# A two-layer H3 convolution and SwiGLU kernel: a list scheduler in the kernel orders all engines, and the first block is transformed without butterflies

## The chip, the cores and the metric

The kernel runs on one core of one Trainium2 chip. The time is the device time of one execution in microseconds (us). The core has five engines with a queue each, which they work off in order: TensorE (PE in the profile; its weight loads are shown apart as PEld), VectorE (DVE), ScalarE (ACT), GpSimd (POOL) and SyncE (SP), which here only starts transfers (DMA). They wait for each other by semaphores. Matmul results land in PSUM, which has eight banks of 128 x 512 fp32; all else lies in SBUF.

## What is computed

Two layers, each a gated long convolution followed by a SwiGLU network, both with a layer norm in front and a sum behind. S is 2048, D is 512, F is 1792, all in bf16. The reference, cut to what matters:

```
def A(q, k, v, shift_k, ssm_k, ssm_D):
    k_shift = causal convolution of k with 4 taps per channel
    kv = k_shift * v
    y = irfft(rfft(pad(kv)) * rfft(pad(ssm_k)))[:S]     # causal convolution over S
    return q * (y + kv * ssm_D)
def B(x, w_gate, w_up, w_down):
    return (silu(x @ w_gate) * (x @ w_up)) @ w_down
x = A_q
x = x + A(layernorm(x), A_k, A_v, ...);  x = x + B(layernorm(x), ...)
x = x + A(layernorm(x), A_k, A_v, ...);  x = x + B(layernorm(x), ...)
```

The convolution y does not depend on x, so it is computed once and used by both layers.

## The kernel before

**Tiles.** The sequence is cut into four blocks of 512 rows (NB), each held as 128 partitions x 4 rows (R). The tokens of a block are worked in two halves of 2 x 128 rows. A *unit* is (layer, block, half); the 16 units run block by block, (0,c,0), (0,c,1), (1,c,0), (1,c,1).

**The convolution** of a block c: hn (the kernel's taps) is transposed on TensorE into hs; the shift convolution is 64 matmuls of kTb with the diagonal taps dg, and VectorE multiplies the result into vt (L216). A transform of hs or vt goes to the frequency domain in two steps: eight sums of two matmuls each with the cosine and sine blocks fwd, evicted by ScalarE into ev (`half`, L160 to L169), and then butterflies of sums and differences on VectorE (L174, L175), which give X (of vt) or H (of hs). G is H combined with the H of the block before. `product` (L224) multiplies X and G in four slots of two parts, into Z. `inverse` (L253) first folds Z by sums and differences into su (L250, L251), then runs four sums of four matmuls with inv, one for each row r, and ScalarE copies them to Yk. Blocks 1 to 3 also need products with earlier blocks.

**A prologue** of a unit (L310): layer norm statistics of xc (L290, L291), ve = variance + eps (L294) and rstd = ve to the power -1/2 (L296) on GpSimd, n (L302), times Yk, added to xc, a second layer norm in the same way, z (L302), and z transposed into zT: by DMA on SyncE's queue (L335), for the very first unit on TensorE (L333).

**A unit's network**: `gate_up` (L343) has 112 matmuls of 256 columns of zT with wg and wu into the PSUM banks pf; ScalarE evicts them to sg (silu) and ht, VectorE multiplies (L358). `down` (L368) has 28 matmuls of ht with wd into two banks pd, which VectorE adds to xc (L380). For layer 1, xc is then stored (L366).

**What sets the order.** Up to the first unit the order of VectorE, ScalarE and TensorE is that of the code. Behind it, the units' loop has a hook, `tick`, after each pair of gate and up tiles: it draws steps from the next units' prologues and from a stream of convolution work, by two accounts of estimated cost (rates 2.8 and 1.2). The framework's own scheduler then places the instructions. Loads of hn and vt of block 0 go by ScalarE's queue, all others by SyncE's. TensorE begins with 36 matmuls of the identity that compute nothing (L459).

Of the kernel before, what the change touches and what calls it, by code (L numbers as in the profile page):

```python
# [18 lines left out]
NB = 4  # L19
R = 4  # L20
# [5 lines left out]
          ("nC", 1, 3), ("nC", 2, 3), ("S", 2, 0), ("S", 3, 0)]  # L26
BI = {(f, r): i for i, (f, r, _) in enumerate(BLOCKS)}


@with_exitstack  # L30
def kernel(
# [20 lines left out]
    N = 2 * L  # L52
    assert L == R * P and D == KD * P and F == NF * P and D <= 512

    q2 = A_q.rearrange("b s d -> (b s) d")
    k2 = A_k.rearrange("b s d -> (b s) d")
    v2 = A_v.rearrange("b s d -> (b s) d")
    o2 = out.rearrange("b s d -> (b s) d")

    q_t = q2.rearrange("(c p r) d -> p c r d", p=P, r=R)  # L60
    v_t = v2.rearrange("(c p r) d -> p c r d", p=P, r=R)
    o_t = o2.rearrange("(c p r) d -> p c r d", p=P, r=R)
    k3 = k2.rearrange("s (dt p) -> s dt p", p=P)
    h3 = A_ssm_k.rearrange("(dt p) s -> p dt s", p=P)


    HP = R // 2
    FG = [range(f, min(f + 4, NF)) for f in range(0, NF, 4)]

    const = tc.alloc_tile_pool(name="const", bufs=1)  # L70
    ldp = tc.alloc_tile_pool(name="ld", bufs=1)
    big = tc.alloc_tile_pool(name="big", bufs=10)
    wp = tc.alloc_tile_pool(name="wts", bufs=1)
    xp = tc.alloc_tile_pool(name="xp", bufs=2)
    small = tc.alloc_tile_pool(name="small", bufs=4)
    work = tc.alloc_tile_pool(name="work", bufs=2)
    psp = tc.alloc_tile_pool(name="psp", bufs=1, space=PSUM)

    PADL = 16
    sig, xs, wts = {}, {}, {}  # L80

    def load_h(b, eng):
        hn = ldp.tile([P, KD, L], BF16, name="hn")
        eng.dma_start(out=hn[:], in_=h3[:, :, b * L:(b + 1) * L])
        sig[b, "h"] = hn

    def load_k(b):
        kTb = ldp.tile([P, KD, PADL + L], BF16, name="kTb")
        if b == 0:
            nc.gpsimd.memset(kTb[:, :, 0:PADL], 0.0)  # L90
            nc.sync.dma_start_transpose(out=kTb[:, :, PADL:PADL + L], in_=k3[0:L])
        else:
            nc.sync.dma_start_transpose(out=kTb[:, :, :], in_=k3[b * L - PADL:(b + 1) * L])
        sig[b, "k"] = kTb

    def load_v(b, eng):
        vt = ldp.tile([P, R, D], BF16, name="vt")
        eng.dma_start(out=vt[:], in_=v_t[:, b])
        sig[b, "v"] = vt

    def load_x(c):
        xc = xp.tile([P, R, D], BF16, name="xc")
        nc.sync.dma_start(out=xc[:], in_=q_t[:, c])
        xs[c] = xc

    def load_weights(which):
        if which in ("g", "u"):
            t = wp.tile([P, KD, F], BF16, name=f"w{which}_sb")
            src = (B_w_gate if which == "g" else B_w_up).rearrange("(k p) f -> p k f", p=P)
        else:  # L110
            t = wp.tile([P, NF, D], BF16, name="wd_sb")
            src = B_w_down.rearrange("(k p) d -> p k d", p=P)
        nc.sync.dma_start(out=t[:], in_=src)
        wts[which] = t

    def psf():
        return psp.tile([P, D], F32, name="pf", bufs=4)

    def psc():
        return psp.tile([P, D], F32, name="pc", bufs=2)  # L120
# [5 lines left out]
    def drain(*gens):  # L126
        for g in gens:
            for _ in g:
                pass

    def together(*gens):
        gens = list(gens)
        while gens:
            for g in list(gens):
                if next(g, gens) is gens:
                    gens.remove(g)


    FWD_TERMS = {
# [5 lines left out]
    NT = len(BLOCKS)  # L145
    fwd = const.tile([P, NT, P], BF16, name="fwd")
    inv = const.tile([P, NT, P], BF16, name="inv")
    ident = const.tile([P, P], BF16, name="ident")
    tapT = const.tile([P, KD, KS], BF16, name="tapT")
    dcol = const.tile([P, KD, 1], BF16, name="dcol")  # L150
    dg = const.tile([P, KD, KS, P], BF16, name="dg")
    nhalf = const.tile([P, 1], F32, name="nhalf")

    def fT(f, r):
        return fwd[:, BI[f, r], :]

    def iT(f, r):
        return inv[:, BI[f, r], :]

    def half(rows, ev, par, scale, ps_of, engines):  # L160
        for key in ("ac", "bd")[par]:
            slot = "abcd".index(key)
            for part in (0, 1):
                ps = ps_of()
                mm(ps[:], [(fT(f, r), rows[:, r, :]) for f, r in FWD_TERMS[key][part]])
                if engines[part] is nc.vector:
                    nc.vector.tensor_scalar(out=ev[:, slot, part], in0=ps[:], scalar1=scale, scalar2=None, op0=ALU.mult)
                else:
                    nc.scalar.activation(out=ev[:, slot, part], in_=ps[:], func=ACT.Copy, scale=scale)  # L169
            yield 0, 0.9  # L170

    def butterfly(ev, dst, sl):
        lo, hi = (slice(0, 2), slice(2, 4)) if sl is None else (sl, sl + 2)
        nc.vector.tensor_tensor(out=dst[:, lo], in0=ev[:, lo], in1=ev[:, hi], op=ALU.add)  # L174
        nc.vector.tensor_tensor(out=dst[:, hi], in0=ev[:, lo], in1=ev[:, hi], op=ALU.subtract)  # L175

    def forward(rows, dst, scale):
        ev = big.tile([P, 4, 2, D], BF16, name="ev", tag="s8")
        for par in (0, 1):
            yield from half(rows, ev, par, scale, psc, (nc.scalar, nc.scalar))  # L180
        butterfly(ev, dst, None)
        yield 2.4, 0

    X, G, H, Y, Z = {}, {}, {}, {}, {}

    def transpose_h(b, ring, order=(0, 2)):
        hn = sig.pop((b, "h"))
        hs = ldp.tile([P, R, D], BF16, name="hs")
        sig[b, "hs"] = hs
        for r0 in order:  # L190
            pt = psp.tile([P, 2, D], BF16, name="pt", tag=ring[0], bufs=ring[1])
            for r in (r0, r0 + 1):
                for dt in range(KD):
                    nc.tensor.transpose(pt[:, r - r0, dt * P:(dt + 1) * P], hn[:, dt, r:L:R], ident[:])
            nc.scalar.copy(out=hs[:, r0:r0 + 2, :], in_=pt[:])  # L195
            yield 0, 0.5

    def spectrum_h(b):
        yield from transpose_h(b, ("pc", 2))
        H[b] = big.tile([P, 4, 2, D], BF16, name="H", tag="s8")  # L200
        yield from forward(sig.pop((b, "hs")), H[b], 2.0 / N)
        G[b] = big.tile([P, 4, 2, D], BF16, name=f"G{b}", tag="s8")
        Hp = H.pop(b - 1)
        nc.vector.tensor_tensor(out=G[b][:, :, 0, :], in0=H[b][:, :, 0, :], in1=Hp[:, :, 1, :], op=ALU.subtract)
# [19 lines left out]
    def product(i, j, sl=slice(0, 4)):  # L224
# [3 lines left out]
        if k not in Z:  # L228
            Z[k] = big.tile([P, 4, 2, D], BF16, name="Z", tag="s8")
# [343 lines left out]
```

## Time and profile before

| | |
|---|---|
| median of 3 runs | 409.09 us (408.4 to 410.74) |
| the profiled execution | 409.77 us |
| its span, first to last instruction | 408.0 us |
| mean granted TensorE clock | 0.97 |
| TensorE busy | 372.0 us |
| VectorE busy | 279.3 us |
| ScalarE busy | 188.9 us |
| GpSimd busy | 41.3 us |

All times that follow from rows are of the profiled execution; its span is 1.8 us below its own time and 1.1 us below the median. In a row of the timeline stand the start, the length, the engine, the line of the kernel, the operation with its tiles and shapes, the count, and in brackets the idle time before it with what ended it. Rows of one engine can overlap a little, since its instructions are pipelined.

### The profile page before, as it was taken

The page shows a single profiled execution, that of the slowest core. Times are in us where ns is not written, and L with a number is a line of the kernel's source. Part 1 is how long each engine was busy: PE and PEld are TensorE (multiplying, and loading weights), DVE is VectorE, ACT ScalarE, POOL GpSimd, SP SyncE. Part 2 cuts the span into 40 slices and gives each one's busy share as a digit, 9 for nine tenths or more (in the row PEclk, how much of TensorE's full clock was granted, in tenths as well). Part 3 has the DMA queues.
Part 4 walks back from the last instruction along what each step waited for, and adds up shares of the span by engine and source line. Part 5 has one row for each costly group of instructions (what it writes and reads, how often), then busy time and mean ns, then how long its engine had stood idle before and what let it go on. Part 6 is the DMA issues. An engine that isn't in the chain of part 4 may idle for free.

```text
span 408.0 us, 6771 instructions
## 1 busy us (share of the span) xinstructions
PE 372.0 (91%) x2808; PEld 266.2 (65%) x2808; DVE 279.3 (68%) x469; ACT 188.9 (46%) x319; POOL 41.3 (10%) x73
## 2 busy tenths in 40 slices
PE   4977699986999999999969989996999999999996
PEld 4832586754767677867646766784767577767773
DVE  5588791987998228978999981597889761445322
ACT  4496236432454553455415436631454444434451
POOL 1100100021011000020121220011010100000000
PEclk9799699998999999999999999998999999999999
DMA  8993030101012320202020112001010020020100
GB/s 213 399 266 129 3 73 20 40 0 27 0 27 52 79 79 0 55 8 71 2 51 2 27 39 66 2 2 26 2 26 27 7 58 17 0 27 0 27 27 26
DMA packets 34351, 20.42 MB, mean 50 GB/s; under 512 B 26384, under 2 KB 32272, under 8 KB 34320
## 3 DMA queue, kind: packets, MB, share of 16 engines
q1 hardware_dynamic: 32592, 18.93, 17.1%
q10 hardware_dynamic: 1728, 1.05, 1.0%
q8 instruction: 22, 0.36, 0.4%
q14 instruction: 9, 0.07, 0.1%
HBM read 11.80 MB, written 2.10 MB: 34 GB/s over the span
## 4 chain that ended last, share of the span: by engine, by line
PE 49%; DVE 32%; POOL 6%; DMA 5%; issue 4%; ACT 4%; ACTq 0%; DVEq 0%
PE pf L124 30%; PE pd L377 12%; PE pc L124 6%; DVE bnst L290 4%; DVE t L236 3%; POOL rstd L296 3%; DVE ht L358 3%; POOL ve L294 3%; DVE t L234 3%; DMA zT<-z 3%; DVE t L243 2%; DVE xc L380 2%; DVE Z L240 2%; DMA hn<-in_A_ssm_k_dram 2%; DVE n L302 2%
## 5 line engine op out<-in xcount | busy, mean ns | idle before, releaser
L355 ACT ACTIVATE sg<-pf 128x512 bf16<-128x512 f32 x112 | 66.9, 597 | 151.7 <-PE pf L124 135.9
L124 PE MATMUL pf<-zT,wg_sb 128*128 128x256 bf16 x896 | 119.4, 276 | 7.4 <-DMA zT<-z 7.4
L124 PE MATMUL pf<-zT,wu_sb 128*128 128x256 bf16 x896 | 118.4, 276 | 0.0
L377 PE MATMUL pd<-wd_sb,ht 128*128 128x512 bf16 x448 | 107.8, 379 | 8.7 <-DVE ht L358 7.0
L124 PEld LDWEIGHTS <-wg_sb 128*128 128x128 bf16 x896 | 88.3, 99 | 34.6 <-issue 5.8
L124 PEld LDWEIGHTS <-wu_sb 128*128 128x128 bf16 x896 | 88.9, 99 | 11.3
L358 DVE TENSOR_TENSOR ht<-ht,sg 128x1024 bf16<-128x1024 bf16 x64 | 39.4, 616 | 62.8 <-ACT ht L356 62.8
L356 ACT CAST ht<-pf 128x512 bf16<-128x512 f32 x112 | 65.7, 586 | 33.1 <-PE pf L124 33.1
L377 PEld LDWEIGHTS <-ht 128*128 128x128 bf16 x448 | 42.9, 98 | 53.3 <-DVE ht L358 10.5
L294 POOL TENSOR_SCALAR ve<-mv 128x2 f32<-128x2 f32 x32 | 17.6, 550 | 336.0 <-DVE mv L291 336.0
L290 DVE BATCH_NORM_STATS2 bnst<-xc 128x6 f32<-128x512 bf16 x64 | 41.5, 677 | 0.3
L380 DVE TENSOR_TENSOR xc<-xc,pd 128x512 bf16<-128x512 bf16 x32 | 20.9, 681 | 16.4 <-PE pd L377 16.4
L169 ACT ACTIVATE ev<-pc 128x512 bf16<-128x512 f32 x48 | 26.6, 600 | 2.9 <-PE pc L124 2.7
L234 DVE TENSOR_TENSOR t<-X,G 128x2048 bf16<-128x2048 bf16 (+1 forms) x22 | 24.6, 1118 | 0.3
L236 DVE TENSOR_TENSOR t<-X,G 128x2048 bf16<-128x2048 bf16 (+1 forms) x22 | 24.6, 1116 | 0.0
L296 POOL TENSOR_TENSOR rstd<-ve,nhalf 128x2 f32<-128x2 f32 x32 | 22.7, 710 | 2.7
L124 PEld LDWEIGHTS <-fwd 128*128 128x128 bf16 x128 | 12.7, 99 | 15.3 <-issue 6.5
L302 DVE TENSOR_SCALAR z<-xc,mv,rstd 128x512 bf16<-128x512 bf16 x32 | 11.8, 410 | 14.7 <-POOL rstd L296 14.7
L302 DVE TENSOR_SCALAR n<-xc,mv,rstd 128x512 bf16<-128x512 bf16 x32 | 11.8, 409 | 11.9 <-POOL rstd L296 11.9
L124 PEld LDWEIGHTS <-kTb 128*128 128x128 bf16 x256 | 17.8, 120 | 0.2
L124 PE MATMUL pc<-hs,fwd 128*128 128x512 bf16 x48 | 14.3, 411 | 1.1 <-ACT hs L195 0.9
L243 DVE TENSOR_TENSOR t<-t,t 128x2048 bf16<-128x2048 bf16 x12 | 14.6, 1215 | 0.1
(62 smaller groups left out, 226.6 us busy)
## 6 DMA issues: line engine op xcount, KB each, us to landing
xc<-in_A_q_dram SPq DMA_DIRECT2D x4, 512.0 KB, 3.8
out_dram<-xc SPq DMA_DIRECT2D x16, 128.0 KB, 1.7
wg_sb<-in_B_w_gate_dram SPq DMA_DIRECT2D x1, 1792.0 KB, 12.2
wu_sb<-in_B_w_up_dram SPq DMA_DIRECT2D x1, 1792.0 KB, 17.7
wd_sb<-in_B_w_down_dram SPq DMA_DIRECT2D x1, 1792.0 KB, 16.0
hn<-in_A_ssm_k_dram SPq DMA_DIRECT2D x3, 512.0 KB, 5.7
vt<-in_A_v_dram SPq DMA_DIRECT2D x3, 512.0 KB, 3.7
hn<-in_A_ssm_k_dram ACTq DMA_DIRECT2D x1, 512.0 KB, 7.7
```

Of the source, the lines that this page charges most:

```text
L124: nc.tensor.matmul(o, lhsT=lhsT, rhs=rhs, start=(n == 0), stop=(n == len(terms) - 1))
L234: nc.vector.tensor_mul(out=t1[:], in0=Xi[:, sl, 0, :], in1=Gj[:, sl, part, :])
L236: nc.vector.tensor_mul(out=t2[:], in0=Xi[:, sl, 1, :], in1=Gj[:, sl, 1 - part, :])
L290: nc.vector.bn_stats(out=st[:], in_=xc[:, HP * h + o, :])
L294: nc.gpsimd.tensor_scalar(out=ve[:], in0=mv[:, :, 1], scalar1=LN_EPS, scalar2=None, op0=ALU.add)
L296: nc.gpsimd.tensor_tensor(out=rstd[:], in0=ve[:], in1=nhalf[:].to_broadcast((P, HP)), op=ALU.pow)
L302: eng.tensor_scalar(out=dst, in0=xc[:, HP * h + o, :], scalar1=mv[:, o, 0:1], scalar2=rstd[:, o:o + 1], op0=ALU.subtract, op1=ALU.mult)
L355: nc.scalar.activation(out=sg[:, o:o + 2, :], in_=pg[:], func=ACT.Silu)
L356: nc.scalar.copy(out=ht[:, o:o + 2, :], in_=pu[:])
L358: nc.vector.tensor_mul(out=ht[:], in0=ht[:], in1=sg[:])
L377: nc.tensor.matmul(pd[:], lhsT=ht[:, q, o * P:(o + 1) * P], rhs=wts["d"][:, ft, :], start=(ft == 0), stop=(ft == NF - 1))
L380: nc.vector.tensor_add(out=xc[:, i, :], in0=xc[:, i, :], in1=pd[:])
```

## The change

The units' loop, `tick`, the stream and the framework's scheduling are taken out. Each step of the whole kernel is now added to a plan as an operation with an engine, an assumed cost, what it reads and writes and, for the network's steps, a due time. A list scheduler inside the kernel (`Plan.order`) lays down all five engines' orders at once, before anything is emitted: it plays the steps through with the assumed costs, takes on each engine the step that can start first, the one due first where several can start, and gives out buffers (rings of tiles by name) as they come free in that play. Due times: unit starts are laid 22 us apart (18 for the last block), from 38 us on; steps ahead get theirs from what waits for them.

Other parts of the change:

- The first block's X is computed without butterflies: `direct` puts the sum or difference into the choice of blocks, with four matmuls for each of eight results. Two more blocks of cosines and sines are held for it (14 in place of 12).
- Its product goes slot by slot: two operations of 1024 columns with one operand broadcast, two of 512.
- Its inverse, `inverse_direct`, has no fold: four PSUM banks (two named pd, two pc) collect 32 single matmuls as slots of Z come.
- ve is computed on VectorE, the power stays on GpSimd.
- The first unit's second layer norm goes row by row.
- The loads of hn and vt of block 0 go by SyncE's queue.
- Where TensorE would stand idle over 0.5 us before 38 us of the play, identity matmuls are put in: 120 in all.

The diff, cut to its core:

```diff
+    def order(self, warm_until, warm):
...
+        while done < len(self.ops):
+            best = None
+            for e, cand in ready.items():
...
+                    key = (max(est, t[e] + self.WAIT[e]), o.due, o.n)
+                    if pick is None or key < pick[0]:
+                        pick = (key, est, o)
+                if pick is not None and (best is None or pick[1] < best[1]):
+                    best = pick
...
+            if e == "PE" and est < warm_until and est - t[e] > 0.5:
+                self.dummy(warm, t[e], est)
...
+            o.emit()
+            o.start, o.end = est, est + o.cost
...
+    def direct(rows, dst, ring, engs):
+        for slot in (0, 2, 1, 3):
+            c1, c2, sign = (("a", "c", 1), ("b", "d", 1), ("a", "c", -1), ("b", "d", -1))[slot]
+            for part in (0, 1):
+                terms = FWD_TERMS[c1][part] + [(f if sign > 0 else NEG[f], r) for f, r in FWD_TERMS[c2][part]]
...
+                add("PE", pe(4), lambda ps=ps, terms=terms: mm(ps.t[:], [(fT(f, r), rows.t[:, r, :]) for f, r in terms]),
+                    r=[rows, fwd], w=[ps])
...
+        if n == 1:
...
+            for t, part in ((t1, 0), (t2, 1)):
+                dve(2 * D, lambda t=t, part=part: nc.vector.tensor_mul(
+                    out=t.t[:], in0=x.t[:, sl, part:part + 1, :].to_broadcast((P, 2, D)), in1=g.t[:, sl]),
...
+    def inverse_direct(k, slots_order):
...
+        pss = [new(("pd", "pd", "pc", "pc")[r], "ps", [P, D], F32) for r in range(R)]
+        for n, slot in enumerate(slots_order):
+            for part in (0, 1):
+                for r in range(R):
...
+                    st, sp = (n == 0 and part == 0), (n == len(slots_order) - 1 and part == 1)
+                    add("PE", pe(1), lambda f=f, q=q, r=r, slot=slot, part=part, st=st, sp=sp: nc.tensor.matmul(
+                        pss[r].t[:], lhsT=iT(f, q), rhs=z.t[:, slot, part], start=st, stop=sp),
...
-        nc.gpsimd.tensor_scalar(out=ve[:], in0=mv[:, :, 1], scalar1=LN_EPS, scalar2=None, op0=ALU.add)
+        add("DVE", 0.08, lambda: nc.vector.tensor_scalar(out=ve.t[:], in0=mv.t[:, :, 1], scalar1=LN_EPS, scalar2=None,
+                                                         op0=ALU.add), r=[mv], w=[ve])
...
+    T0, DF, DC = 38.0, 18.0, 22.0
...
+    plan.dues({"DVE": 2.0, "PE": 3.0, "ACT": 1.0, "POOL": 1.0, "SP": 1.0}, T0 + 2)
...
+        plan.order(T0, warm)
```

Three places show how the instructions move. The first is SyncE's queue at the start of the program, with its first loads. Before:

```order
L91 DMA_TRANSPOSE kTb<-in_A_k_dram 128x4x512
L103 DMA xc<-in_A_q_dram 128x2048
L113 DMA wg_sb<-in_B_w_gate_dram 128x4x1792
L113 DMA wu_sb<-in_B_w_up_dram 128x4x1792
L84 DMA hn<-in_A_ssm_k_dram 128x4x512
```

And in the same place of the changed kernel, where the first hn and vt are among them:

```order
L280 DMA_TRANSPOSE kTb<-in_A_k_dram 128x4x512
L274 DMA hn<-in_A_ssm_k_dram 128x4x512
L289 DMA vt<-in_A_v_dram 128x2048
L300 DMA wg_sb<-in_B_w_gate_dram 128x4x1792
L293 DMA xc<-in_A_q_dram 128x2048
L300 DMA wu_sb<-in_B_w_up_dram 128x4x1792
```

xc has moved from second place to fifth, behind hn, vt and wg; the hn of the first rows above is that of block 1.

The second place is VectorE in the first block: X, G and Z are its spectra, t the two halves of a product. Before:

```order
L174 TENSOR_TENSOR X_308<-evx 128x1024
L175 TENSOR_TENSOR X_308<-evx 128x1024
L234 TENSOR_TENSOR t_386<-X_308,G_309 128x1024
L236 TENSOR_TENSOR t_387<-X_308,G_309 128x1024
L240 TENSOR_TENSOR Z<-t_386,t_387 128x2x512
L234 TENSOR_TENSOR t_422<-X_308,G_309 128x1024
L236 TENSOR_TENSOR t_423<-X_308,G_309 128x1024
L240 TENSOR_TENSOR Z<-t_422,t_423 128x2x512
L250 TENSOR_TENSOR su<-Z 128x1024
L251 TENSOR_TENSOR su<-Z 128x1024
```

And the end of the same stretch in the changed kernel, up to the first prologue:

```order
L435 TENSOR_TENSOR t_503<-X_440,G_420 128x1024
L439 TENSOR_TENSOR Z<-t_465,t_476 128x512
L439 TENSOR_TENSOR Z<-t_483,t_494 128x512
L435 TENSOR_TENSOR t_520<-X_440,G_420 128x1024
L439 TENSOR_TENSOR Z<-t_483,t_494 128x512
L439 TENSOR_TENSOR Z<-t_503,t_520 128x512 x2
L553 TENSOR_TENSOR n<-n,Yk 128x512 x2
```

The butterflies of X and the folds to su are gone, and the products stand slot by slot.

The third place is VectorE from the end of the first unit's down projection, in the prologue of unit (1,0,0). Before:

```order
L380 TENSOR_TENSOR xc<-xc,pd 128x512 x2
L290 BN_STATS bnst<-xc 128x6 x2
L291 BN_AGGR mv<-bnst 128x2
L240 TENSOR_TENSOR Z<-t_1002,t_1003 128x4x512
L291 BN_AGGR mv<-bnst 128x2
L234 TENSOR_TENSOR t_1097<-X_742,G_309 128x2048
L302 TENSOR_SCALAR n<-xc,mv,rstd 128x512 x2
L358 TENSOR_TENSOR ht<-ht,sg 128x1024
L320 TENSOR_TENSOR n<-n,Yk 128x1024
L236 TENSOR_TENSOR t_1098<-X_742,G_309 128x2048
L321 TENSOR_TENSOR xc<-xc,n 128x1024
L243 TENSOR_TENSOR t_1097<-t_1097,t_1098 128x2048
```

And in the changed kernel:

```order
L612 TENSOR_TENSOR xc<-xc,pd 128x512 x2
L511 BN_STATS bnst<-xc 128x6 x2
L512 BN_AGGR mv<-bnst 128x2 x2
L600 TENSOR_TENSOR ht<-ht,sg 128x1024
L514 TENSOR_SCALAR ve<-mv 128x2
L446 TENSOR_TENSOR t_1042<-X_440,G_681 128x2048
L522 TENSOR_SCALAR n<-xc,mv,rstd 128x512 x2
L543 TENSOR_TENSOR n<-n,Yk 128x1024
L544 TENSOR_TENSOR xc<-xc,n 128x1024
L511 BN_STATS bnst<-xc 128x6 x2
L512 BN_AGGR mv<-bnst 128x2 x2
```

Of four products of 2048 columns between the sum and the second statistics, one is left; ve is a row of VectorE now.

More of the change, by code (lines that the diff above doesn't have):

```diff
@@ L184 @@
[L184 to L204, printed above, removed]
-        yield 1.2, 0
-        nc.vector.tensor_tensor(out=G[b][:, :, 1, :], in0=H[b][:, :, 1, :], in1=Hp[:, :, 0, :], op=ALU.add)
-        yield 1.2, 0
@@ new lines, with run, conv @@
+    spectrum_h(1, "pf")
+    inverse_direct(0, (0, 2, 1, 3))
+    prologue(0, 0, 0, True)
+    prologue(0, 0, 1)
+    T0, DF, DC = 38.0, 18.0, 22.0
+    start = {}
+    t = T0
+    order = [(layer, c, h) for c in range(NB) for layer in (0, 1) for h in range(HP)]
+    for unit in order:
+        start[unit] = t
+        t += DC if unit[1] < NB - 1 else DF
+    def run(unit):
+        ffn(unit, start[unit], DC if unit[1] < NB - 1 else DF)
+    def conv(c):
+        if c >= NB:
+            return
+        if c > 1:
+            spectrum_h(c)
+        spectrum_x(c)
+        load_x(c)
+        if c + 1 < NB:
+            load_h(c + 1)
+            load_k(c + 1)
+            load_v(c + 1)
+        product(0, c)
+        product(c, 0)
+        inverse(c)
```

911 lines of the change are left out of this document (522 added, 389 removed), and 4 rows, old and new, of the table INV_TERMS.

## The prediction

> **What bounds the kernel now.** I read the page first, then the chain of work that ended last, then the timeline, and last the windows in which TensorE stood idle. The page's first part:
>
> ```profile
> span 408.0 us, 6771 instructions
> PE 372.0 (91%) x2808; PEld 266.2 (65%) x2808; DVE 279.3 (68%) x469; ACT 188.9 (46%) x319; POOL 41.3 (10%) x73
> ```
>
> TensorE (PE) looks nearly full, but a modelled busy time hides slow stretches. So I price its work by pieces of the chain that ran without a gap (start, length, count):
>
> ```profile
> 54.15 0.89 PE pc L124 x16
> 55.05 1.75 PE pf L124 x16
> 56.79 0.89 PE pc L124 x16
> 57.69 1.73 PE pd L377 x8
> ```
>
> That is 0.056 us for a matmul of 128 columns, 0.109 for 256, 0.216 for 512. From the first gate matmul on, the kernel of before runs 1792 of 256 (195.4 us), 448 of 512 for the down projections (96.9) and, for the later blocks' convolutions, 208 of 128 (11.6) and 128 of 512 (27.7): 331.6 us. Between which times?
>
> ```profile
> 46.48 1.92 PE L124 MATMUL pf<-zT,wg_sb 128*128 128x256 bf16 x8
> ...
> 403.90 1.28 DVE L380 TENSOR_TENSOR xc<-xc,pd 128x512 bf16<-128x512 bf16 x2 [1.11 <-PE pd L377]
> ```
>
> The gate starts at 46.5; VectorE (DVE) takes up the last sum at 403.9, so the matmuls end there: 357.4 us for 331.6 of work. The span is a ramp of 46.5, work of 331.6, **25.8 lost**, and a tail of 4.1 that stays. The losses are gaps such as these and slow restarts behind them (after the range: its length, then each engine's busy time, PE first, DVE third):
>
> ```profile
> 80.00:100.00 20.00, 15.09 (x98) 9.90 (x97) 18.08 (x29) 4.86 (x9) 4.83 (x5) 0.93 0.07 14
> 200.00:220.00 20.00, 15.86 (x107) 10.00 (x106) 18.57 (x29) 7.17 (x13) 3.62 (x4) 1.00 0.10 26
> 260.00:280.00 20.00, 17.23 (x155) 12.98 (x153) 18.19 (x31) 6.27 (x11) 3.08 (x4) 1.00 0.04 8
> ```
>
> In each, TensorE misses 3 to 5 us while VectorE is over 90% busy; over the span VectorE is at 68%. It serves convolution products while a prologue that TensorE needs stands in line: a matter of order, not of amount.
>
> **The ramp.** Before:
>
> ```profile
> 21.24 3.63 PE L124 MATMUL pf<-vt,fwd 128*128 128x512 bf16 x16
> 22.12 4.07 ACT L169 ACTIVATE evx<-pf 128x512 bf16<-128x512 f32 x8
> ...
> 24.26 0.69 DVE L174 TENSOR_TENSOR X<-evx 128x1024 bf16<-128x1024 bf16 x1 [0.67 <-ACT evx L169]
> ...
> 36.94 0.68 DVE L251 TENSOR_TENSOR su<-Z 128x1024 bf16<-128x1024 bf16 x1
> ```
>
> From 24.26 to 37.62 VectorE runs 20 operations of 1024 columns, 0.67 us apart. The change takes away four butterflies of X and four folds (8 x 0.67 = 5.3 us), and gives TensorE 16 more forward and 16 more inverse matmuls (32 x 0.216 = 6.9 us). The product becomes, for each of four slots, two operations of 1024 columns (0.61 each, the step inside a run of such rows) and two of 512 (0.37, half of this row): about 2.0 us, 8.0 in all.
>
> ```profile
> 43.48 0.73 DVE L302 TENSOR_SCALAR z<-xc,mv,rstd 128x512 bf16<-128x512 bf16 x2 [1.14 <-POOL rstd L296]
> ```
>
> A slot of X takes TensorE 8 x 0.216 = 1.73 us, less than VectorE's 2.0, so the added forward matmuls lie beside VectorE but for the first slot: 1.73, and 0.8 until it is evicted, 2.5. The inverse matmuls follow as slots come; only the last two of the first two rows are on the path.
>
> When can the direct transform start? It needs vt multiplied, and here the loads matter (last column: from issue to landing):
>
> ```profile
> 2.19 0.74 SPq L103 DMA_DIRECT2D xc<-in_A_q_dram  x1
> ...
> 2.99 0.41 SPq L113 DMA_DIRECT2D wg_sb<-in_B_w_gate_dram  x1
> ```
> ```profile
> wg_sb<-in_B_w_gate_dram SPq DMA_DIRECT2D x1, 1792.0 KB, 12.2
> ...
> xc<-in_A_q_dram SPq DMA_DIRECT2D x1, 512.0 KB, 8.4
> ```
>
> xc landed at 10.6, wg at 15.2. Now xc stands behind hn, vt and wg on one queue; the five first loads are the same 3.9 MB, so I put xc near 14.8, where wg ended. VectorE has three statistics of xc ahead of the first vt multiply, and waits there.
>
> ```profile
> 18.81 1.25 DVE L216 TENSOR_TENSOR vt<-pf,vt 128x512 bf16<-128x512 f32 x2
> ```
> ```profile
> 78.40 1.20 DVE bnst L290 x2
> ```
>
> Four statistics (0.60), four multiplies (0.62), two n (0.37) and small ones make 5.9 us: vt is done at 20.7, against 20.1 before. The h transform's evictions (0.51 each) run behind it to about 22.9. So 22.9 + 2.5 + 8.0, less 0.4 since the last slot waits for TensorE: **Z is done at 33.0**, against su at 37.6. From su to the gate before took 8.9 us. Now: two matmuls and evictions 1.3, multiply and add by row 1.4, two statistics and ve 1.7, two powers 1.7, z, transposes and eviction 1.3, together 7.4. **The gate starts at 40.4, a gain of 6.1.**
>
> Both ends of what no row shows: xc landing at 10.6 brings 3.5 us; a broadcast operand that halved the product's rate would cost eight times 0.53, 4 us. The dummy matmuls, 113 now ahead of hn's transposes, are the third:
>
> ```profile
> 1.72 2.95 PE L459 MATMUL pf<-ident 128*128 128x128 bf16 x26 [1.72 <-POOL ident masks.py:199]
> ```
> ```profile
> 4.25 1.16 PE L459 MATMUL pf<-ident 128*128 128x128 bf16 x12
> ```
>
> At the first row's pace, 0.106 us, they hold TensorE to 13.7, 4 us too long; in the second the pace is 0.08 and falling. At 0.056 from 4.9 on they end at 9.5, when hn's transposes began before. I take 9.5, as the later row is nearer to what follows.
>
> **The units.** After the gate TensorE has 332.9 us of work by the same prices (16 shift and two inverse matmuls more). How much of the 25.8 comes back? A layer-1 unit's gate waits for a chain: the down projection two units earlier, the add to xc, two layer norms, a transpose by DMA.
>
> ```profile
> 77.12 1.27 DVE L380 TENSOR_TENSOR xc<-xc,pd 128x512 bf16<-128x512 bf16 x2
> ...
> 96.05 1.03 PE L124 MATMUL pf<-zT,wg_sb 128*128 128x256 bf16 x8 [2.17 <-DMA zT<-z]
> ```
> ```profile
> 192.18 1.28 DVE L380 TENSOR_TENSOR xc<-xc,pd 128x512 bf16<-128x512 bf16 x2
> ...
> 211.02 1.03 PE L124 MATMUL pf<-zT,wg_sb 128*128 128x256 bf16 x8 [1.24 <-DMA zT<-z]
> ```
>
> Both took 18.9 us, and in both the order puts 13.6 us of VectorE work between add and second z: a chain needs its VectorE work and 5.2. TensorE's work between that down projection and the gate, counted in the order, is the room. Before, for the eight layer-1 units: room 14.8, 19.1, 17.4, 15.4, 16.6, 16.5, 13.9, 13.9; VectorE work 13.6, 14.2, 9.6, 13.6, 16.0, 8.5, 7.9, 7.9. What is missing is 4.0, 0.3, 0, 3.4, 4.6, 0, 0, 0, in sum 12.3, and 25.8 were lost: about twice, with restarts and the other units in it. Now: room 15.7, 18.3, 13.9, 16.5, 17.4, 15.7, 15.7, 15.7; work 10.4, 12.7, 10.4, 10.4, 11.5, 10.4, 8.1, 8.1. Missing is 1.7 in one unit; five others fit with under 1 us to spare. Twice 1.7, and 1.6 for the tight ones: **5 us lost in place of 25.8.** The ends are 0 and all of 25.8.
>
> Loads on SyncE (SP) were read for waits: a load that waits for its buffer stands ahead of zT transposes in four places, but its buffer is freed over 10 us of TensorE work ahead of those gates, so it costs nothing; if TensorE came later than its order says, the gate would move with it.
>
> ve moves from GpSimd (POOL) to VectorE, 33 times 0.1 us there. Beside a product it had cost more:
>
> ```profile
> 48.21 0.22 POOL L294 TENSOR_SCALAR ve<-mv 128x2 f32<-128x2 f32 x1 [4.77 <-DVE mv L291]
> ...
> 80.96 1.16 POOL L294 TENSOR_SCALAR ve<-mv 128x2 f32<-128x2 f32 x1 [31.74 <-DVE mv L291]
> 82.20 0.71 POOL L296 TENSOR_TENSOR rstd<-ve,nhalf 128x2 f32<-128x2 f32 x1
> ```
>
> The slow ve began 0.14 us behind a product of 1.2 and ended with it. Now the power stands in that place: in 10 of 33 the row behind ve is a product. I take it that the power is held as ve was: the 5.2 has that in it, so nothing is gained, and where nothing holds it some 0.3 a norm is hidden. If it is not held, the 5 us fall to about 2. The Trainium skill, GPSIMD Engine Reference, section Key points, says that GpSimd shares its SBUF interfaces with VectorE and contends with its instructions of two SBUF inputs; the slow row agrees, and by that rule the sum stays at 5 us lost, against 2 without it.
>
> **Sum.** 40.4 + 332.9 + 5 + 4.1 = 382.4 us of span. The profiled execution of before took 409.77 for 408.0, and the median is 409.09, 1.1 above the span: 383.5.
>
> **Rivals.** (1) *The waits stay.* The order is laid by assumed costs, and an engine that comes late holds its whole queue. For it: five rooms with under 1 us to spare. Against: the four chains that had been too long have 12 us less work. All 25.8 lost gives 404.3; half, 391. (2) *The ramp gains less*, by the late xc, slow dummies or the broadcast: gate at 44.4, 387.5; all of it at 46.5, 389.6. (3) *Slower: the power is locked out by a run of products, not one.* If GpSimd got in only when VectorE pauses, each of 33 powers could wait another 1.14 us, 38 us, and the time would be 421; it ends above 409 from 0.78 us each on. Against it: the slow ve ended with one product, and VectorE itself stops for rstd. (4) *Nothing*: rooms and ramp gains cancel, 407 to 411.
>
> **How the numbers follow.** Forecast 377 to 387: 0.57. Ramp rival, 387 to 391: 0.15. Waits stay, 391 to 407: 0.21. No change: 0.03. Slower: 0.04. So faster by over 0.5% (about what a measurement of this kernel can tell from no change) 0.93, same 0.03, slower 0.04. The range 376 to 399 holds forecast, ramp rival and the lower half of the waits, a little over 8 in 10; its low end has an early xc and under 2 us lost.
>
> **What would show it.** First gate matmul near 40, Z done near 33, and bnst of xc late in the ramp, waiting for a DMA; windows behind the gate with TensorE gaps of some us in all, and no wait over 2 us for zT; gate to last matmul near 338 us. A gate after 44, or a wait of ht or zT in every unit, would make it wrong.

## The result, and the profile after

The changed kernel took 388.21 us (median of 4 runs, 387.24 to 389.45) against 409.29 us for the kernel before in the same comparison: a ratio of 0.948, 95% interval 0.9445 to 0.9522. The forecast was 383.5 us, in a range of 376 to 399. The profiled execution took 387.24 us, its span 385.5 us; the mean granted TensorE clock rose from 0.970 to 0.995.

The page's first part; TensorE does not do much less (the transforms cost more matmuls), it idles less:

```profile
span 385.5 us, 6975 instructions
PE 369.3 (96%) x2883; PEld 268.6 (70%) x2926; DVE 282.7 (73%) x504; ACT 189.1 (49%) x320; POOL 35.7 (9%) x42
```

The same three windows of 20 us as before, with the engines' busy times in the same order. Where TensorE missed 3 to 5 us, it now misses 0.4 to 0.5, although VectorE is fuller than it was (the worst window behind the gate is now that from 100 to 120 us, in which TensorE misses 1.5):

```profile
80.00:100.00 20.00, 19.57 (x153) 14.87 (x153) 19.28 (x28) 9.13 (x17) 2.87 (x2) 1.00 0.07 14
200.00:220.00 20.00, 19.62 (x149) 13.88 (x150) 18.62 (x32) 11.91 (x20) 2.45 (x3) 1.00 0.11 27
260.00:280.00 20.00, 19.50 (x146) 14.29 (x147) 19.76 (x33) 9.01 (x16) 3.65 (x3) 1.00 0.07 14
```

The timeline of the changed kernel, cut to the steps of the ramp and the last sum:

```profile
1.73 8.53 PE L733 MATMUL wm<-ident 128*128 128x128 bf16 x113 [1.73 <-POOL ident masks.py:199]
...
16.57 1.29 DVE L511 BATCH_NORM_STATS2 bnst<-xc 128x6 f32<-128x512 bf16 x2 [4.73 <-DMA xc<-in_A_q_dram]
...
21.82 0.68 DVE L395 TENSOR_TENSOR vt<-ps,vt 128x512 bf16<-128x512 f32 x1
...
24.98 7.07 PE L252 MATMUL ps<-vt,fwd 128*128 128x512 bf16 x32
...
31.40 1.29 DVE L435 TENSOR_TENSOR t<-X,G 128x1024 bf16<-128x1024 bf16 x2
...
33.88 1.09 DVE L439 TENSOR_TENSOR Z<-t,t 128x512 bf16<-128x512 bf16 x3
...
37.96 3.62 PE L252 MATMUL ps<-hs,fwd 128*128 128x512 bf16 x15
41.41 0.39 PE L564 MATMUL ptz<-ident,z 128*128 128x128 bf16 x4
...
43.15 1.04 PE L252 MATMUL pf<-zT,wg_sb 128*128 128x256 bf16 x8
...
381.38 1.28 DVE L612 TENSOR_TENSOR xc<-xc,pd 128x512 bf16<-128x512 bf16 x2 [1.12 <-PE pd L607]
```

Set against the forecast: xc lands at 16.5 (14.8 forecast), vt is done at 22.5 (20.7), the direct transform starts at 25.0 (22.9), Z is done at 35.0 (33.0), the gate starts at 43.15 (40.4). From the gate to the end of the matmuls it is 338.2 us, where I had said "near 338". Forecast and measured span differ by 3.1 us (382.4 and 385.5), and 2.75 of it is the late gate; the median lies 2.7 above the span, where I had allowed 1.1. The broadcast operand runs at the full rate (1.29 us for two).

To compare kernels whose scheduler moves work across the first gate, I use one account for all runs below: **loss** = end of the matmuls, less the start of the gate, less the work behind the gate (matmuls counted in each kernel's order, at 0.056, 0.109 and 0.216 us). Before it was 403.9 − 46.5 − 331.6 = 25.8; now 381.4 − 43.15 − 332.9 = 5.3, where 5 was forecast.

| kernel | median us | gate | work behind it | end | loss |
|---|---|---|---|---|---|
| before | 409.3 | 46.5 | 331.6 | 403.9 | 25.8 |
| the change | 388.2 | 43.15 | 332.9 | 381.4 | 5.3 |
| e1_xc_first | 383.6 | 40.8 | 331.6 | 377.7 | 5.3 |
| e2_x_butterfly | 389.3 | 47.1 | 330.7 | 383.1 | 5.3 |
| e3_no_direct | 392.8 | 54.6 | 328.4 | 388.4 | 5.4 |
| e4_ve_pool | 391.7 | 44.5 | 332.5 | 386.2 | 9.2 |
| e5_double_stats | 413.9 | 44.25 | 332.9 | 407.75 | 30.6 |
| e6_no_due | 413.5 | 50.7 | 330.7 | 407.7 | 26.3 |
| e7_short_warm_h1 | 382.2 | 39.4 | 331.6 | 376.3 | 5.3 |
| e8_short_warm | 387.4 | 43.3 | 332.9 | 381.5 | 5.3 |
| e9_ht_due | 385.15 | 39.4 | 331.6 | 379.3 | 8.3 |
| e10_pow_cost | 379.8 | 39.2 | 331.6 | 373.9 | 3.1 |

What is left of the loss is not where I had put it. The waits of TensorE in the changed kernel (microseconds in all, times, longest) hold none for zT:

```profile
PE pd L607 <- DVE ht L600: 4.2, 6, 1.3
PE ps L252 <- DVE vt L395: 4.1, 3, 3.4
```

The second is the ramp's. The first is the largest part of the loss that a wait shows: down projections that wait for the multiply of ht on VectorE. Its 4.2 us are an upper bound, since this profile holds 422 of the 448 down projection matmuls and a missing one lengthens the wait that it stands beside. The profile of e1_xc_first holds all 448: there these waits come to 2.3 us, and 0.7 more are waits for ScalarE's part of ht, at the same loss of 5.3. So some 2 us of the loss stand in no wait for another engine, and their cause is open.

### The profile page after: what moved, and what is told of

It reads as the page before. It is cut to its first block, busy times and chain, and to the rows that moved or that the text cites. A ratio compares the mean times of both kernels' runs of the same rounds, so it can differ in the third digit from the quotient of the medians.

```text
span 385.5 us, 6975 instructions
## 1 busy us (share of the span) xinstructions
PE 369.3 (96%) x2883; PEld 268.6 (70%) x2926; DVE 282.7 (73%) x504; ACT 189.1 (49%) x320; POOL 35.7 (9%) x42
## 4 chain that ended last, share of the span: by engine, by line
PE 53%; DVE 38%; DMA 3%; POOL 3%; issue 1%; SPq 1%; ACT 1%; DVEq 0%; POOLq 0%
PE pf L252 27%; PE pd L607 14%; PE ps L252 9%; DVE bnst L511 6%; DVE ht L600 4%; DVE t L449 4%; DMA xc<-in_A_q_dram 3%; DVE t L446 3%; POOL rstd L516 3%; DVE xc L612 3%; DVE t L458 2%; DVE n L522 2%; DVE Z L460 2%; PE ps L499 2%; DVE Z L455 1%; DVE n L543 1%
## 5 line engine op out<-in xcount | busy, mean ns | idle before, releaser
L252 PE MATMUL pf<-zT,wu_sb 128*128 128x256 bf16 x896 | 116.1, 273 | 0.0
L252 PE MATMUL pf<-zT,wg_sb 128*128 128x256 bf16 x896 | 116.1, 273 | 0.0
L607 PE MATMUL pd<-wd_sb,ht 128*128 128x512 bf16 x422 | 102.4, 379 | 6.0 <-DVE ht L600 4.2
L516 POOL TENSOR_TENSOR rstd<-ve,nhalf 128x2 f32<-128x2 f32 (+1 forms) x33 | 34.6, 1049 | 319.4 <-DVE ve L514 319.4
L322 ACT ACTIVATE ev<-ps 128x512 bf16<-128x512 f32 x56 | 31.6, 604 | 21.4 <-PE ps L252 14.9
L612 DVE TENSOR_TENSOR xc<-xc,pd 128x512 bf16<-128x512 bf16 x32 | 20.5, 683 | 19.3 <-PE pd L607 19.3
L449 DVE TENSOR_TENSOR t<-X,G 128x2048 bf16<-128x2048 bf16 x18 | 21.9, 1219 | 0.0
L446 DVE TENSOR_TENSOR t<-X,G 128x2048 bf16<-128x2048 bf16 x18 | 21.9, 1218 | 0.0
L252 PE MATMUL ps<-hs,fwd 128*128 128x512 bf16 x58 | 16.7, 401 | 4.2 <-DVE vt L395 4.1
L252 PE MATMUL ps<-vt,fwd 128*128 128x512 bf16 x74 | 19.7, 379 | 0.2
L252 PE MATMUL ps<-dg,kTb 128*128 128x128 bf16 x256 | 16.1, 219 | 0.0
L252 PEld LDWEIGHTS <-kTb 128*128 128x128 bf16 x256 | 15.5, 114 | 0.5
```

The source lines that it names most:

```text
L252: nc.tensor.matmul(o, lhsT=lhsT, rhs=rhs, start=(n == 0), stop=(n == len(terms) - 1))
L322: add("ACT", act(D), lambda: nc.scalar.activation(out=view(), in_=ps.t[:], func=ACT.Copy, scale=scale), r=[ps], w=[(buf, keys)], conv=conv)
L446: dve(n * D, lambda t1=t1, part=part: nc.vector.tensor_mul(out=t1.t[:], in0=x.t[:, sl, 0, :], in1=g.t[:, sl, part, :]), [(x, key(slots, (0 ...
L449: dve(n * D, lambda t2=t2, part=part: nc.vector.tensor_mul(out=t2.t[:], in0=x.t[:, sl, 1, :], in1=g.t[:, sl, 1 - part, :]), [(x, key(slots ...
L516: add("POOL", 0.75, lambda: nc.gpsimd.tensor_tensor(out=rstd.t[:], in0=ve.t[:], in1=nhalf.t[:].to_broadcast((P, n)), op=ALU.pow), r=[ve, n ...
L607: nc.tensor.matmul(pds[o].t[:], lhsT=ht.t[:, q, o * P:(o + 1) * P], rhs=wt["d"].t[:, ft, :], start=(ft == 0), stop=(ft == NF - 1))
```

## The experiments

All are edits of the changed kernel. Medians are compared with its 388.2 us, or with that of the run they build on.

### Is the late gate the late xc?

```diff
-        add("SP", 0.6, lambda: nc.sync.dma_start(out=wt[which].t[:], in_=src), w=[wt[which]], lat=12.0)
+        add("SP", 0.6, lambda: nc.sync.dma_start(out=wt[which].t[:], in_=src), w=[wt[which]], lat=12.0,
+            slack=-8.0 if which in "gu" else 0.0)
```

The weights wg and wu get later due times, so xc of block 0 is issued ahead of wg.

> Only the queue of the first loads changes: xc of block 0 is issued ahead of wg (1792 KB). Theory (the ramp came out 2.75 us late because xc landed at 16.5, and its statistics stand on VectorE ahead of the first multiply into vt): xc lands before 12, its statistics no longer wait, vt is done 4 to 5 us earlier than the changed kernel's 22.5, the first gate matmul starts near 38.5 (range 37.5 to 40) and the time falls by 3 to 5.5 us, to about 383.5; the stretch from the gate to the last matmul stays at 338 +- 1. Rival 1 (the transform of h on TensorE and its evictions hold the direct transform anyway): vt earlier, but the first gate within 1 us of 43.15 and the time within 1 us. Rival 2 (wg, now behind xc, lands late and holds the gate): the first gate waits for wg, no gain or a loss up to 2 us.

Its timeline:

```profile
10.74 0.69 DVE L512 BATCH_NORM_STATS2 bnst<-xc 128x6 f32<-128x512 bf16 x1 [2.27 <-DMA xc<-in_A_q_dram]
...
19.62 7.07 PE L252 MATMUL ps<-vt,fwd 128*128 128x512 bf16 x32
...
29.09 0.64 PE L375 MATMUL pt<-ident,hn 128*128 128x128 bf16 x8 [1.10 <-DMA hn<-in_A_ssm_k_dram]
...
40.81 1.04 PE L252 MATMUL pf<-zT,wg_sb 128*128 128x256 bf16 x8
```

383.6 us (383.54 to 383.69): 4.6 us faster, and the forecast's own time. xc is there at 10.7 in place of 16.5 and the direct transform starts 5.4 us earlier, so the late xc did hold the ramp. The gate came 2.3 us earlier, at 40.8, outside the expected 37.5 to 40, mainly for two reasons: 0.9 us of shift matmuls (16 of 128 columns) now stand ahead of it, and TensorE waits 1.1 us for hn of block 1. The loss stayed at 5.3.

```diff
-                    n = int((b - a - 0.2) / 0.062)
+                    n = int((b - a - 0.2) / 0.09)
```

> The changed kernel with 77 dummy matmuls in place of 113 ahead of hn's transposes (82 in place of 120 in all), nothing else. Theory (late xc covers the dummies: VectorE waits for xc until 16.5 whatever TensorE does): hn's transposes start about 2 us earlier and the first gate and the time stay within 0.7 us of the changed kernel's 43.15 and 388.2. Rival (the dummies hold the ramp): 1.5 to 2 us faster.

This is the changed kernel with fewer dummy matmuls. 387.38 us (387.01 to 388.4), so 0.8 us less in the median, with ranges that overlap; the gate is at 43.29 and the span 385.6, the same. hn's transposes began at 8.48 in place of 10.32, and the gain went into a longer wait of the h transform for VectorE, which reads the shift convolution's results into vt only after the statistics of xc: 5.27 us, where it had been 3.39.

```profile
19.44 0.59 PE L252 MATMUL ps<-hs,fwd 128*128 128x512 bf16 x1 [5.27 <-DVE vt L395]
```

So the dummies cost nothing here: xc covers them. With xc early, they could have counted:

```diff
# on top of e1_xc_first
-                    n = int((b - a - 0.2) / 0.062)
+                    n = int((b - a - 0.2) / 0.09)
...
-        add("SP", 0.6, ..., w=[wt[which]], lat=12.0,
+        add("SP", 0.6, ..., r=[hn[1]] if which == "d" else (), w=[wt[which]], lat=12.0,
...
+    load_h(1)
     load_weights("d")
-    load_h(1)
```

> As e1_xc_first, with two more edits in the ramp: 77 dummy matmuls ahead of hn's transposes in place of 113, and the load of wd behind that of hn of block 1 (in e1_xc_first TensorE waited 1.1 us for that hn). Theory (with xc early, TensorE bounds the ramp up to the direct transform: it ran from 9.75 to 26.5 with 0.2 us of idle, and hn was there at 8.3): hn's transposes start near 8.4, the direct transform 1 to 2 us earlier, no wait for hn of block 1, time 1.5 to 3 us below e1_xc_first's 383.6, so 380.6 to 382.1. Rival (VectorE's statistics and multiplies, without a gap from 10.7 to 17.3 there, bound it): under 1 us.

```profile
11.73 0.94 PE L659 MATMUL it<-ident,fwd 128*128 128x128 bf16 x14 [1.37 <-DVE hs L382]
...
19.54 7.07 PE L252 MATMUL ps<-vt,fwd 128*128 128x512 bf16 x32
```

382.19 us: 1.4 us below e1_xc_first, between the two expectations. The direct transform did not move (19.54 against 19.62): TensorE now waits 1.37 us for a copy of hs that stands behind the statistics of xc on VectorE. So the gain goes to the other edit, hn of block 1, whose wait of 1.1 us is gone; the two edits were not run apart.

### What are the first block's edits worth?

```diff
-    direct(vt[0], X[0], "pf", ("ACT", "ACT"))
+    for par in (0, 1):
+        half(vt[0], evx, par, 1.0, "pf", ("ACT", "ACT"), False)
+        butterfly(evx, X[0], par, False)
```

> Block 0's X is again made by eight sums of two matmuls and butterflies on VectorE; product by slots and unfolded inverse stay as in the changed kernel. Theory (VectorE bounds the ramp, TensorE's added matmuls lie beside it): four butterflies of X, 8 operations... of which four pairs' 0.67 us each come back: between four and eight such operations ahead of Z, less the 1.73 us that the first slot's eight matmuls took and 16 forward matmuls less, so the first gate is later by 2 to 4 us (43.15 to 45.2-47.2) and the time 390.2 to 392.2. Rival (TensorE, which ran without a gap from 25.0 to 32.1 there, bounds it): 16 fewer matmuls of 0.216 make the gate earlier by up to 3.5 us, time 385 to 388.

```diff
# besides, in place of inverse_direct
+    for par in (0, 1):
+        ... nc.vector.tensor_add(out=su0.t[:, par:par + 1], in0=z0.t[:, par:par + 1], in1=z0.t[:, par + 2:par + 3])
+        ... nc.vector.tensor_sub(out=su0.t[:, par + 2:par + 3], in0=z0.t[:, par:par + 1], in1=z0.t[:, par + 2:par + 3])
+    for r in range(R):
+        ... mm(psr.t[:], [(iT(f, q), su0.t[:, sl_, part]) for f, q, sl_, part in INV_TERMS[r]])
```

> As e2_x_butterfly, and block 0's inverse is folded again: four sums and differences into su on VectorE, then four sums of four matmuls. So this is the list scheduler without both edits of the first block's arithmetic. Theory (the two edits are worth the ramp only, and the scheduler alone brings the units' gain): first gate 5 to 8 us later than 43.15, that is 48 to 51, gate to last matmul 338 +- 1.5, time 393 to 396. Rival (the ramp's gain is of the order too): gate within 3 us of 43.15, time below 391.

With the butterflies of X back, the gate is at 47.06, 3.9 us later and in the range; the time is 389.3, only 1.1 us longer and below the expected 390.2 to 392.2 (the ranges of the two kernels overlap: 388.97 to 389.65 against 387.24 to 389.45). With the folded inverse as well, the gate is at 54.58, past the range, and the time 392.8, 4.6 us longer and just below the range. Both times I had counted the gate's delay as lost. The scheduler fills it: in e2 32 and in e3 64 shift matmuls of block 1, and two of its transform in e3, stand ahead of the gate, and the arithmetic needs fewer matmuls (3.5 and 6.9 us in all). The loss behind the gate is 5.3 and 5.4. So of the 21.1 us that the change gained, the two edits of the first block bring 4.6 (X 1.1, the inverse 3.5), and 16.5 come from the rest: the scheduler with its due times, ve, the loads and the dummies together.

### Does a layer-1 chain have room to spare?

```diff
-            add("DVE", 0.6, ... nc.vector.bn_stats(out=st.t[:], in_=xs[c].t[:, i, :]), ...
+            add("DVE", 0.6, ... [nc.vector.bn_stats(out=st.t[:], in_=xs[c].t[:, i, :]) for _ in range(times)], ...
```

`times` is 2 in the prologues of layer 1; the orders are the same on every engine.

> Each layer-norm statistic of the layer-1 prologues is computed twice in place (8 prologues x 4 operations x 0.6 us = 19 us more on VectorE, which is 73% busy); the order on all engines is the same. Each layer-1 chain from the down projection to the gate is 2.4 us longer. Theory (a chain needs its VectorE work and 5.2 us, and the room that the order leaves is full to within 1 us in six of eight units): shortfall 2.3, 2.0, 4.1, 1.5, 1.7, 2.3, 0, 0 us, in sum 14 and 12 more than in the changed kernel; waits for zT appear in front of layer-1 gates and the time rises by 9 to 20 us, to 397-408. Theory with a smaller constant (no wait for zT showed, so the need is about 1.5 to 3 us less than I said): +3 to +8 us, 391 to 396. Rival (VectorE has the time to spare, the room is not what counts): under +2 us.

413.9 us: 25.7 more, above every expectation. VectorE, which was 73% busy, is busy for 22.3 us more (282.7 to 305.0), not for the 19 that I had put. The waits of TensorE name one cause, and it is not zT:

```profile
PE pd L607 <- DVE ht L600: 23.5, 16, 3.3
```

The timeline in the last block, where the order left most room:

```profile
357.16 2.75 DVE L511 BATCH_NORM_STATS2 bnst<-xc 128x6 f32<-128x512 bf16 x4
...
359.82 0.30 DVE L512 BATCH_NORM_AGGREGATE mv<-bnst 128x2 f32<-128x6 f32 x2
360.16 0.17 DVE L514 TENSOR_SCALAR ve<-mv 128x2 f32<-128x2 f32 x1
360.24 0.68 DVE L600 TENSOR_TENSOR ht<-ht,sg 128x1024 bf16<-128x1024 bf16 x1
...
360.98 1.41 PEld L607 LDWEIGHTS <-ht 128*128 128x128 bf16 x8 [1.45 <-DVE ht L600]
360.98 1.90 PE L607 MATMUL pd<-wd_sb,ht 128*128 128x512 bf16 x8 [1.17 <-DVE ht L600]
```

The multiply of ht stands in VectorE's queue behind the prologue's statistics, and the down projection waits for it. Every statistic that is done twice delays it. Here the statistics take 2.66 us up to the aggregate (357.16 to 359.82), in the same place of the changed kernel 1.21 (352.89 to 354.10): 1.45 us were added, and the weight load waits 1.45. Over the run I count the waits of the weight loads for ht, since all 448 are recorded in both profiles: they rose from 6.8 to 29.8, by 23.0 us for the 22.3 added. (The matmuls' waits rose by 19.3, from the 4.2 that is an upper bound.) A smaller part is the clock: behind the gate of the changed kernel it is 1.00 in every window up to 380 us, here it is 0.95, 0.93 and 0.96 in the windows of 20 us from 260 to 320, 3.2 us in sum. The gate came 1.1 later. So the room that I had counted between down projection and gate is not what decides. A chain is paid for at the next ht in line.

### What do the due times bring, and what the move of ve?

```diff
-                    key = (max(est, t[e] + self.WAIT[e]), o.due, o.n)
+                    key = (max(est, t[e] + self.WAIT[e]), o.n)
```

> The scheduler picks by the time at which a step can start, and among equals by its place in the program, with no due times. The network's multiplies of ht and the convolution's products of later blocks then stand in another order on VectorE: all of the convolutions' work comes earlier. It also brings xc ahead of wg in the first loads, as in e1_xc_first. Theory A (the gain of the units comes from the playing-through of all engines in one plan; due times are a detail): gate to last matmul loses 5 to 8 us as in the changed kernel, time 383 to 388. Theory B (the due times keep the products out of the way of the prologues and of ht): the loss behind the gate goes back to 15 to 30 us, waits of TensorE for ht or zT over 10 us in sum, time 393 to 410.

413.5 us, above even theory B's range; the loss is 26.3, about that of the kernel before (25.8), and the gate is at 50.7 (part of the time comes from there). Without due times, VectorE runs the convolutions in one stretch, in the timeline from 148.9 to 166.8 with not one ht, and TensorE waits for what comes late in it, the folded sums su (first the timeline of VectorE, then of TensorE, then a row of the waits):

```profile
148.25 0.69 DVE L600 TENSOR_TENSOR ht<-ht,sg 128x1024 bf16<-128x1024 bf16 x1
...
166.76 0.69 DVE L600 TENSOR_TENSOR ht<-ht,sg 128x1024 bf16<-128x1024 bf16 x1
```
```profile
162.23 1.01 PE L252 MATMUL ps<-su,inv 128*128 128x512 bf16 x2 [6.13 <-DVE su L477]
```
```profile
PE ps L252 <- DVE su L477: 10.0, 3, 6.1
```

I had named waits for ht or zT as its mark; ht has 3.1 us and zT none. So one plan for all engines that goes by the order of the program among steps that can start equally early brings nothing behind the gate; the gain there hangs on the due times.

```diff
-        add("DVE", 0.08, lambda: nc.vector.tensor_scalar(out=ve.t[:], ...), r=[mv], w=[ve])
+        add("POOL", 0.22, lambda: nc.gpsimd.tensor_scalar(out=ve.t[:], ...), r=[mv], w=[ve])
```

> ve goes back from VectorE to GpSimd under the list scheduler (the plan charges 0.22 us there); all else as the changed kernel, though the scheduler lays the order anew. Theory (behind a product of two operands either ve or the power is held, so the move brought the time of one free ve, about 0.3 us a norm, and no more): some ve rows behind products take 0.9 to 1.2 us again, the powers behind them fall back to 0.7, and the time is 0 to 2.5 us longer than the changed kernel's 388.2. Rival (each GpSimd step beside products pays for itself: 33 norms lose up to 0.9 us each, and the double statistics showed that each us of such a chain is paid in full): +5 to +15 us.

391.7 us (390.74 to 392.08): 3.5 more, between the two expectations, and the loss is 9.2, 3.9 more. The scheduler laid the order anew, so this is the price of the move together with its order. A norm of this run, from its timeline:

```profile
167.40 1.19 DVE L460 TENSOR_TENSOR Z<-Z,t 128x2048 bf16<-128x2048 bf16 x1
167.57 1.10 POOL L514 TENSOR_SCALAR ve<-mv 128x2 f32<-128x2 f32 x1 [36.94 <-DVE mv L512]
...
168.51 1.22 DVE L446 TENSOR_TENSOR t<-X,G 128x2048 bf16<-128x2048 bf16 x1
168.75 1.54 POOL L516 TENSOR_TENSOR rstd<-ve,nhalf 128x2 f32<-128x2 f32 x1
...
170.33 0.73 DVE L522 TENSOR_SCALAR n<-xc,mv,rstd 128x512 bf16<-128x512 bf16 x2 [0.60 <-POOL rstd L516]
```

ve is held to the end of one product (168.59) and done 0.1 us behind it; the power is held to the end of the next (169.73) and done 0.56 behind that. I had taken it that one step of a norm is held, ve or the power, so that the move gains nothing. Both are: here ve has a mean of 603 ns and the power 1014, and in the changed kernel the power alone has 1049. The waits of VectorE in front of n and z show it too, first this run, then the changed kernel:

```profile
DVE z L522 <- POOL rstd L516: 10.7, 15, 1.1
DVE n L522 <- POOL rstd L516: 10.5, 13, 1.1
```
```profile
DVE n L522 <- POOL rstd L516: 8.1, 12, 0.9
DVE z L522 <- POOL rstd L516: 4.9, 7, 0.9
```

That is 21.2 us against 13.0. Waits for zT, which the changed kernel has none of, come back with 2.2 us in 3:

```profile
PE pf L252 <- DMA zT<-z: 2.2, 3, 0.8
```

### Can the last 5 us be had?

```diff
# each on top of e7_short_warm_h1; e9:
-            dve(n * W, lambda sg=sg, ht=ht: ..., [sg], [ht], due=t0 + k * step)
+            dve(n * W, lambda sg=sg, ht=ht: ..., [sg], [ht], due=t0 + k * step - 4.0)
# e10:
-        add("POOL", 0.75, lambda: nc.gpsimd.tensor_tensor(out=rstd.t[:], ..., op=ALU.pow), ...)
+        add("POOL", 1.3, lambda: nc.gpsimd.tensor_tensor(out=rstd.t[:], ..., op=ALU.pow), ...)
```

> As e7_short_warm_h1, but the multiplies of ht get due times 4 us earlier, so that the scheduler sets them ahead of other VectorE steps where both can start. By the order, room and VectorE work of the layer-1 chains are now 14.3/9.8, 17.4/12.7, 14.3/9.8, 13.9/12.7, 15.2/10.9, 13.9/10.4, 13.9/7.5, 13.9/8.1. Room rule of the prediction (a gate needs the chain's work and 5.2): 8.5 us missing in six units where 1.7 were, so waits for zT and +7 to +15 us: 389 to 397. Rival (what TensorE waits for is ht, whose multiply stands behind a prologue's statistics in VectorE's queue; a gate has more to spare than 5.2 says): the 4.2 us of waits for ht fall to under 2, and the time to 379 to 381.5. Third (both: ht earlier, zT later, about even): within 1 us of 382.2.

385.15 us, 3.0 more than e7_short_warm_h1: none of the three. Waits for ht fell only from 4.2 to 3.4 (those of the weight loads from 6.8 to 5.8), zT came to 1.5 and a transform's vt to 1.4. The last unit's down projections were left in one piece of 20 at the end (11 in e7_short_warm_h1); whether that costs anything is not shown. The room rule's 7 to 15 us are refuted as a size, and so is an earlier due time for ht as a cure.

> As e7_short_warm_h1, but the plan's assumed cost of the power on GpSimd is 1.3 us in place of 0.75 (measured: mean 1.05, 1.5 to 1.6 behind a product). Nothing else; the order follows. Theory (the 4.2 us of waits for ht come from chains that are longer than the plan assumes, mostly by the held power): with the truer cost the waits fall to 1 to 3 us and the time to 379.5 to 381.5. Room rule of the prediction (room/work now 16.1/11.5, 19.1/12.7, 16.1/11.5, 13.9/11.5, 17.0/11.5, 15.7/11.5, 15.7/8.1, 15.7/8.1: 5 us missing): +3 to +8 us. Rival (the plan is far enough off elsewhere that one cost does not matter): within 1 us of 382.2.

379.80 us (379.61 to 379.97), 2.4 less than e7_short_warm_h1, as the theory had it; the room rule had asked for 3 to 8 more. The waits for ht fell from 4.2 to 1.1 (those of the weight loads from 6.8 to 4.0) and the loss from 5.3 to 3.1:

```profile
PE pd L608 <- DVE ht L601: 1.1, 3, 0.6
```

The plan had charged 0.75 us for a power that takes 1.05 in the mean. With 1.3, near the 1.5 to 1.6 beside a product, it lays more of other work between ve and n: VectorE's idle time in front of n and z falls from 13.0 to 7.5 us. This is the fastest kernel of the study: a ratio of 0.9305 to the kernel before, interval 0.9272 to 0.9339.

## Why the prediction came out right, point by point

Direction and range were right, and the size to 4.7 us. The time lies 1.2 us above the 387 at which I had cut the likeliest case, in the stretch of the second rival, the ramp that gains less.

The chain of unit (1,1,0) in the changed kernel, from the sum behind the down projection to the first gate matmul, and then z in the first chain that the prediction shows of the kernel before:

```profile
161.46 1.28 DVE L612 TENSOR_TENSOR xc<-xc,pd 128x512 bf16<-128x512 bf16 x2
...
171.57 0.73 DVE L522 TENSOR_SCALAR z<-xc,mv,rstd 128x512 bf16<-128x512 bf16 x2
...
175.92 1.03 PE L252 MATMUL pf<-zT,wg_sb 128*128 128x256 bf16 x8
```
```profile
91.72 0.73 DVE L302 TENSOR_SCALAR z<-xc,mv,rstd 128x512 bf16<-128x512 bf16 x2 [0.91 <-POOL rstd L296]
```

- **The units.** "5 us lost in place of 25.8": 5.3 measured. The sum was right by luck, its make-up was not. I had 1.7 us of missing room in unit (1,1,0), doubled, and 1.6 for tight rooms, all as waits for zT. There were none; up to 4.2 us are waits for ht. The step that failed is "a chain needs its VectorE work and 5.2". In that unit the gate started 14.5 us behind the sum, with no wait, for 10.4 us of VectorE work: the need is 4.1 at most. From the end of z to the gate it is 3.6 us in both chains shown; what has gone is VectorE's wait for the power, 0.9 us in front of n and of z each in the chain of before and none here, because ht and products now fill it. And the room up to the gate is not the nearest limit: e5 shows that the next ht in VectorE's queue is. One error asked for too much, the other left a wait out, and they about cancelled. e9 and e10, which went 3.0 and −2.4 us where the rule asked for 7 to 15 and 3 to 8 more, show that it could not have been carried further.
- **ve.** "Nothing is gained": 3.5 us are, by e4 (3.9 in the loss), order included. The mechanism that I took from the slow ve of before is right, a GpSimd step is held to the end of a VectorE product; that only one step of a norm meets it is wrong.
- **The ramp.** A gain of 6.1 us was forecast and 3.3 came. The term that was mis-sized is the landing of xc: 16.5 in place of 14.8. I had put it where wg ended before, but the rows that I showed for wg (issued at 2.99, 12.2 us to landing) say 15.2; and xc, issued at 4.05, landed over 1 us later still. With it early (e1) the whole time is the forecast one, though the gate is then at 40.8 with 0.9 us of other work ahead of it. Of the 2.75 us, 2.0 stand at Z already. The steps from Z to the end of z took 6.1 us; from z, done at 41.0, to the gate it took 2.1, where the 7.4 in all had left 1.3: TensorE ran block 1's h transform up to 41.4 before it took the transposes.
- **The bounds.** Broadcast operand: no cost, as taken. Dummies: they ended at 10.3, not 9.5, and cost nothing since xc came later (e8). An xc at 10.6 was priced at 3.5 us; e1, with xc at 10.7, gained 3.7 in the span and 4.6 in the median.
- **Butterflies and folds.** "5.3 us" of VectorE gone against 6.9 us of matmuls: worth 4.6 us of time in all, X only 1.1 of it, which the runs hardly tell from nothing.
- **The rivals.** *The waits stay* did not happen, but it hangs on the due times: by e6 the same scheduler without them loses 26.3 us. *The ramp gains less* is what happened, in part, and by the late xc as it said: 387.5 with a gate at 44.4 was its price, 388.2 with a gate at 43.15 the result. *Slower* is refuted for this order: no power took over 1.6 us beside products of 1.2. *Nothing* is refuted by the time; and e3 adds that the scheduler's gain does not need the new arithmetic.

What stays open is the last 3.1 us of e10_pow_cost: 1.1 are waits for ht, the other 2.0 were not traced, and about as much is left over in e1_xc_first.

## What to carry to other kernels

Where one engine's queue serves both a long prologue and the short steps that the busiest engine waits for, look for the short step that stands behind the prologue: here the prologue was paid for there, one to one, long before its own result was late, on an engine that was 73% busy on average. A planner is as good as its due times and its costs: look up in the trace what each step takes in company, not alone, and give it that. And count a ramp by the work that TensorE has not done by its end, not by when a named step starts, since a scheduler moves work across that mark.

## What the hardware showed beyond that

- A GpSimd step that starts while a VectorE operation with two inputs in SBUF runs is held by it. In e4_ve_pool ve (0.22 us alone) is done 0.1 us behind that operation and the power (0.7 alone) 0.55 to 0.57 behind it, whatever its length, and the next step is held anew; in the changed kernel the power took 1.0 to 1.1 beside ht's multiply of 0.6 and 1.5 to 1.6 beside a product of 1.2. Beside a statistic of xc, which has one input, it took 0.7. The Trainium skill, GPSIMD Engine Reference, section Key points, has the contention with such instructions; these rows agree and give it a size.
- SyncE's queue can be held by the issue of a load. In the changed kernel that of xc of block 1, behind three weights, took 12.2 us, and hn of block 1 went out only at 19.0:

```profile
6.64 12.20 SPq L293 DMA_DIRECT2D xc<-in_A_q_dram  x1
19.01 1.92 SPq L274 DMA_DIRECT2D hn<-in_A_ssm_k_dram  x1
```

- A long wait costs TensorE more than its length. In e6_no_due, behind the wait of 6.1 us for su, the window from 160 to 180 us has a granted clock of 0.87; in the changed kernel, with no wait over 1.4 us behind the gate, it is 1.00 in every such window up to 380 us. The Trainium skill, TensorE: Matmul & The Clock Gate, Part 1, says that the array falls to half speed after an idle window of about 3.4 us; the two runs agree with it. As a limit on a single wait it does not hold here: in e5_double_stats the clock is 0.95 and 0.93 in the windows from 260 to 300, whose longest waits are 2.28 and 2.32 us, and 1.00 from 100 to 120, beside a wait of 3.34.
